# A DeltaNet and max-out kernel on one core: the fourth query tile in a buffer of its own, negations shared by two engines, unread products in the opening, and a last output tile in two halves

## The chip, the cores and the metric

The kernel runs on one core of one Trainium2 chip. The metric is the device time of one execution in microseconds (us), taken as the median of several runs. A profile of one further execution shows what each engine did: PE is TensorE (the matmul engine; PEld is its weight load), DVE is VectorE, ACT is ScalarE, POOL is GpSimd, and SP is the engine that here only starts transfers. A name with a q (SPq, ACTq, POOLq) is the engine's instruction queue at work, mostly starting a transfer (DMA).

## What is computed

```python
# attention block: 4 batches, 8 heads, 768 steps, head size 48
k_n = k / (np.linalg.norm(k, axis=-1, keepdims=True) + 1e-06)
for t in range(S):
    y[:, :, t] = np.einsum('bhd,bhde->bhe', q[:, :, t], state)
    v_old = np.einsum('bhde,bhd->bhe', state, kt)
    state = state + bt[:, :, :, None] * np.einsum('bhd,bhe->bhde', kt, vt - v_old)
# bridge: (B,H,S,D) -> (3072 tokens, 384)
h = np.maximum(np.maximum(x @ w1, x @ w2), x @ w3)     # 384 -> 768
return h @ w_out                                       # 768 -> 384
```

All data is float32. The recurrence over time is strictly sequential; the second block needs the outputs of the first.

## The kernel before

**Tiling.** The 768 steps are cut into 12 chunks of 64 (`NCH`), two chunks make one of six groups (`GROUPS`), and a group gives 512 tokens (`TOK`) for the max-out block. The keys and queries of a chunk come as two tiles n (`load_k(n)`, `load_q(n)`, each two transfers). `turn(n, parts)` transposes a key tile (part 0) or a query tile (part 1) on PE through an identity matrix (L342) and evicts it with one copy (L348, mostly ACT). `gram(n, parts)` multiplies keys with keys or with queries (L419) and evicts with a copy (L430 or L436).

**Recurrence.** Within a chunk the steps are turned into a triangular system. `solve(m)` inverts its diagonal blocks for a whole group on DVE, a long alternation of two small operations (L571, L575). For the first group it ends with a DVE transpose (L583) and copies of the result into the tile `ut` (`placed`, L509), on DVE and ACT. Then PE and the eviction engines alternate for chunk 0: `halves_t` (DVE transposes, L655 and L657), `halves_z` (PE product p_e, copies L698), `halves_u` (PE p_f, negations L710), `turn_t1` (DVE transposes L640, L642), `join_z` (PE p_z, copies L727), `join_u` (PE p_j, negations L738), `new` (PE p_u, copies L786), `to_y` (PE p_y, copies L827), `to_x` (PE p_x, copies L849). For chunk 0 each of these works in two halves of four heads, so that one half is evicted while PE works on the other. `negated_of` names the PSUM tiles and the engine of each negation; for chunk 0 it gives the first half to ACT alone and the second to ACT and DVE, so of the eight negations L710 ACT has six and DVE two, and of the four negations L738 ACT has three and DVE one. `masked` multiplies a `gram` result with the causal mask on DVE (L403). `placed(1, i)` writes the result for chunk 1.

**Max-out block.** `ffn(m)` yields after each small piece; the main loop (L1478, L1531) puts the recurrence of the next group, weight conversion (`weights`: three ACT operations L251 to L253, DVE L263, POOL L267 a piece) and transfers between those pieces. The last groups use fast schemes with fewer products (`crossed_hidden`, `outputs`).

**Order.** All orders are written out by hand (`manual_schedule`), each engine works strictly in the order of the program text, and waits for others by semaphores. The opening is the list of calls from L1314 to L1393. Three query slots exist (`NQ`, the tile `qall`), so `load_q(3)` writes the slot of query tile 0: its transfer stands on POOL's queue behind the first copy of the solve (L546) and waits for `turn(0, (1,))`. `busy(n, of)` (L1306) is already in the kernel: n products of the 128 by 128 identity with itself whose result nobody reads, six before the first transposes, two after `to_y(0)`, one after `to_x(0)`.

**Ending.** `outputs(5, ...)` makes the last four quarter results. The last lines accumulate `p` in eight products and evict it (L1106, stored by SP, L1107), then `q` in two products, evict it (L1110) and store it on both queues (L1111). A store is two transfers of 96 KB.

Of the kernel before, what the change touches and what calls it, by code (L numbers as in the profile page):

```python
# [16 lines left out]
C = 64  # L17
# [6 lines left out]
def kernel(  # L24
# [93 lines left out]
    def rows(bb):  # L118
        return slice(C * bb, C * (bb + 1))
# [18 lines left out]

    def load_k(n, queues=one_queue):
        load(k, kpad[place(n)], n, queues)  # L140

    def load_q(n, queues=one_queue):
        load(q, qpad[n % NQ], n, queues)

    def load_v(c, queue=nc.sync):
        vts[c] = work.tile([128, 2, H, D], FP32, name="v_t", bufs=3)
# [179 lines left out]
    def turn(n, parts=(0, 1), copy=nc.scalar.copy):  # L326

        if n not in kqts:
            if n == 6:
                kqts[n] = work.tile([128, KT, TOK], FP32, name="xt").rearrange(  # L330
                    "p k t -> p (k t)"
                )[:, 0 : NP * 4 * C].rearrange(
                    "p (j b i t) -> p j b i t", b=2, i=2, t=C
                )
            else:
                kqts[n] = work.tile([128, NP, 2, 2, C], FP32, name="kqt", bufs=6)
        kqt = kqts[n]
        p_t = ps_two("p_t")
        for i in parts:
            src = (kpad[place(n)], qpad[n % NQ])[i]  # L340
# [330 lines left out]
    def negated_of(c, name, w):  # L671
        if c:
            p_v = ps_two(name)[:, :, 0 : H * w].rearrange("p g (h x) -> p g h x", x=w)
            yield range(H), (p_v, p_v), (nc.scalar.mul,) * 2
            return
        p = [
            ps_two(name)[:, :, 0 : NP * w].rearrange("p g (h x) -> p g h x", x=w)
            for _ in range(3)
        ]
        yield range(NP), (p[0], p[0]), (nc.scalar.mul,) * 2  # L680
        yield range(NP, H), (p[1], p[2]), (nc.scalar.mul, nc.vector.tensor_scalar_mul)

    def span(hs):
        return slice(hs[0], hs[-1] + 1)
# [294 lines left out]
    def outputs(m, hs):  # L979
# [12 lines left out]
        def times(to, a, b, start=True, stop=True):  # L992
            for g in range(2):
                for j in range(len(a)):
                    nc.tensor.matmul(  # L995
                        to[:, g], a[j][:, 128 * g : 128 * (g + 1)], b[j],
                        start=(start and g == j == 0),
                        stop=(stop and g == 1 and j == len(a) - 1),
                    )

        def x_times(to, lo, right, start=False, stop=True):
            times(
                to,
                [xt[:, KT - 1, lo : lo + 256]],
                [w_sb[0][:, KT - 1, HALF * right : HALF * (right + 1)]],
                start, stop,
            )

        def held(name, dtype_bufs):
# [90 lines left out]
        store(m6, 0, 1)  # L1100
        op(m5, m5, m7, plus)
        yield
        times(p, a22, w["t4"], True, False)
        yield
        x_times(p, 256, 0)
# [2 lines left out]
        yield  # L1108
        x_times(q, 256, 1, True)
        op(m5, m5, q, plus)  # L1110
        store(m5, 1, 1, both_queues)  # L1111
        yield

    thirds, x_sums = {}, {}

    def cross_hidden(i):

# [17 lines left out]
    def crossed_hidden(m, hs):  # L1135

        banks = upper_pool("banks")
        xt, vec = xts[m], nc.vector.tensor_tensor  # L1140
        plus = vec if m == GROUPS - 1 else nc.gpsimd.tensor_tensor
        lo, hi = slice(0, 256), slice(256, 512)
# [153 lines left out]

    conv = weights()
    solving = solve(0)
    zeros(*(t[:, :, :, D:DP] for t in kmore), qall[:, :, :, D:DP])
    for t in (*ut, st):  # L1300
        nc.vector.memset(t, 0.0)
    warm = small("warm", 1)
# [35 lines left out]
    to_blocks(3, (V, A, V, P))  # L1338
    first_blocks()
    load_q(2, (nc.gpsimd, nc.gpsimd))  # L1340
    turn(4, (0,))
    turn(5, (0,))
    some(solving, 1)
    keys(4)
    keys(5)
    turn(6, (0,))
    turn(0, (1,))
    load_q(3, (nc.gpsimd, nc.gpsimd))
    load_beta()
# [228 lines left out]
```

## Time and profile before

| What | Value |
|---|---|
| Median of 3 runs | 502.94 us (501.11 to 507.12) |
| Profiled execution, its own time | 501.88 us |
| Its span, first to last instruction | 500.1 us |
| PE busy | 480.0 us, 96% |
| DVE, ACT, POOL busy | 353.0, 168.3, 189.4 us |
| Mean clock granted to PE | 0.97 |
| Share of PE in the chain that ended last | 85% |

The profile's page gives busy times by engine and the span in 40 slices of 12.5 us. A view by stretches gives the same for stretches of one's own choice with the clock that PE was granted (PEclk, 1.00 is full). A timeline lists instructions in order of time, with the idle time before them in brackets and what ended it. The records of PE count two for each float32 product and one for each transpose.

### The profile page before, as it was taken

Reading aid. Unit: us, or ns where it says so; the run is one execution under the profiler, and the core shown is the slowest. Engines: PE = TensorE matmul, PEld = TensorE weight load, DVE = VectorE, ACT = ScalarE, POOL = GpSimd, SP = SyncE. Lnnn points to the kernel's source line nnn. Section 1 sums busy time; section 2 is a strip of 40 time slices with the busy share of each in tenths; the row PEclk is TensorE's granted clock in tenths of the full one; section 3 lists DMA queues with packets and bytes.
Section 4 is the critical chain, followed back from the end, with each engine's and each line's share of the span. In section 5 each row is a group of like instructions: output and inputs, shape, how many; then the busy total and the mean of one; then the engine's idle time right before and its main releaser. Section 6 shows DMA issues by size and latency. Waiting matters only on the chain.

```text
span 500.1 us, 18762 instructions
## 1 busy us (share of the span) xinstructions
PE 480.0 (96%) x8100; PEld 343.7 (69%) x8100; DVE 353.0 (71%) x829; ACT 168.3 (34%) x323; POOL 189.4 (38%) x313
## 2 busy tenths in 40 slices
PE   7779799999999999999999999999999999999996
PEld 6668678878665555565555565565797457998896
DVE  5888999658697352979552998565998864468753
ACT  5576675985330152200243100252211032213210
POOL 7425596764670394780585870601000020000000
PEclk9657999999999999999999999999999999999999
DMA  8936989873351655544775552833223230330002
GB/s 113 196 64 203 200 171 170 199 208 90 81 144 30 138 122 107 145 130 92 147 138 128 137 135 66 171 54 93 65 68 85 55 72 19 86 91 0 1 16 49
DMA packets 110083, 53.51 MB, mean 107 GB/s; under 512 B 93233, under 2 KB 103889, under 8 KB 110001
## 3 DMA queue, kind: packets, MB, share of 16 engines
q1 hardware_dynamic: 98368, 31.91, 31.7%
q0 software_dynamic: 9088, 19.72, 15.8%
q8 instruction: 64, 1.05, 0.9%
q10 hardware_dynamic: 2544, 0.69, 0.8%
q14 instruction: 19, 0.15, 0.1%
HBM read 39.17 MB, written 13.11 MB: 105 GB/s over the span
## 4 chain that ended last, share of the span: by engine, by line
PE 85%; DMA 6%; ACT 3%; POOL 2%; issue 1%; SPq 1%; DVE 1%; POOLq 0%; ACTq 0%; DVEq 0%
PE p_h L1235 32%; PE p_o L1278 13%; PE p_o L995 13%; PE p_c L1173 5%; PE p_g L419 4%; PE p_u L781 2%; PE p_m L915 2%; PE p_y L823 2%; PE p_k L753 2%; DMA kmore<-in_k_dram 2%; PE p_q L753 2%; PE p_s L804 2%; PE p_j L736 2%; PE p_z L723 1%; DMA qall<-in_q_dram 1%
## 5 line engine op out<-in xcount | busy, mean ns | idle before, releaser
L1235 PE MATMUL p_h<-xt,w_sb 128*128 128x512 f32 (+1 forms) x468 | 176.6, 520 | 1.2 <-POOL w_sb L267 0.8
L1235 PEld LDWEIGHTS p_h<-xt,w_sb 128*128 128x128 f32 x468 | 84.5, 190 | 62.4 <-issue 52.8
L1249 DVE TENSOR_TENSOR h<-h,p_h 128x512 f32<-128x512 f32 (+1 forms) x42 | 23.9, 569 | 54.1 <-PE p_h L1235 51.6
L575 DVE TENSOR_TENSOR y_bl<-y_bl,tmp 128x31 f32<-128x31 f32 (+20 forms) x139 | 50.3, 362 | 4.8
L1278 PE MATMUL p_o<-wo_sb,h 128*128 128x384 f32 x144 | 49.2, 490 | 0.4 <-POOL wo_sb L267 0.4
L571 DVE TENSOR_TENSOR tmp<-x_bl,y_bl 128x31 f32<-128x31 f32 (+20 forms) x139 | 45.9, 331 | 4.1
L377 POOL DMA_DIRECT2D turned<-in_q_dram x72 | 39.1, 551 | 5.5 <-POOL turned L372 2.6
L1245 ACT ACTIVATE h<-p_h 128x512 f32<-128x512 f32 (+1 forms) x30 | 16.6, 552 | 70.6 <-PE p_h L1235 70.5
L1278 PEld LDWEIGHTS p_o<-wo_sb,h 128*128 128x128 f32 x144 | 26.8, 190 | 18.5 <-POOL wo_sb L267 1.0
L267 POOL TENSOR_TENSOR w_sb<-mant,up 128x384 int32<-128x384 int32 x18 | 18.7, 1044 | 34.7 <-DVE mant L263 23.7
L419 PEld LDWEIGHTS p_g<-kqt 48*64 48x64 f32 x1216 | 25.1, 145 | 9.8 <-issue 7.6
L419 PE MATMUL p_g<-kqt 48*64 48x64 f32 (+1 forms) x1216 | 28.5, 245 | 0.9 <-ACT kqt L348 0.8
L1284 ACT COPY o_sb<-p_o 128x384 f32<-128x384 f32 x12 | 5.8, 479 | 61.7 <-PE p_o L1278 54.4
L372 POOL MEMSET turned<- 128x96 f32 x18 | 3.3, 190 | 59.2 <-DVE kqt L393 59.2
L608 POOL DMA_DIRECT2D ut<-y_d x4 | 2.6, 650 | 60.4 <-DMA y_d<-y_bl 60.4
L148 POOL DMA_DIRECT2D v_t<-in_v_dram x14 | 11.6, 830 | 28.7 <-PE p_u L781 28.7
L811 DVE TENSOR_TENSOR st<-st,p_s 48x768 f32<-48x768 f32 (+1 forms) x18 | 17.1, 950 | 7.5 <-PE p_s L804 7.1
L403 DVE TENSOR_TENSOR pt<-p_g,mask 128x512 f32<-128x512 f32 x20 | 13.7, 690 | 10.4 <-PE p_g L419 10.3
L1278 PE MATMUL p_o<-w_sb,xt 128*128 128x384 f32 x60 | 21.0, 486 | 0.0
L765 DVE TENSOR_TENSOR v_t<-v_t,p_k 128x768 f32<-128x768 f32 x11 | 10.5, 950 | 13.8 <-PE p_k L753 13.3
L436 ACT COPY at<-p_g 128x512 f32<-128x512 f32 x22 | 12.8, 585 | 18.5 <-DVE pt L403 16.4
L781 PEld LDWEIGHTS p_u<-v_t,ut 64*64 64x64 f32 x768 | 13.7, 141 | 7.2 <-issue 6.1
(240 smaller groups left out, 916.5 us busy)
## 6 DMA issues: line engine op xcount, KB each, us to landing
w_bits<-in_moe_w_dram SPq DMA_DIRECT2D x9, 384.0 KB, 6.7
w_bits<-in_moe_w_dram POOLq DMA_DIRECT2D x9, 384.0 KB, 4.9
turned<-in_q_dram POOLq DMA_DIRECT2D x72, 48.0 KB, 2.6
out_dram<-o_sb SPq DMA_DIRECT2D x36, 96.0 KB, 2.3
y_x<-y SPq DMA_DIRECT2D x32, 96.0 KB, 2.4
qall<-y_x SPq DMA_DIRECT2D x32, 96.0 KB, 2.8
v_t<-in_v_dram POOLq DMA_DIRECT2D x14, 192.0 KB, 4.4
at_d<-at SPq DMA_DIRECT2D x76, 32.0 KB, 2.5
```

What stands on the lines that cost most here:

```text
L267: nc.gpsimd.tensor_tensor(out=dst.bitcast(I32), in0=mant_v.bitcast(I32), in1=up_v, op=ALU.add)
L377: (queue, nc.gpsimd)[i].dma_start(out=t[p0 : p0 + 32, bb, at : at + NP * 2 * D].rearrange("p (j x) -> p j x", j=NP), in_=(k, q)[i][2 * bb ...
L419: nc.tensor.matmul(p_g[rows(bb ^ (g * i)), par, c0 : c0 + C * (1 + whole)], kq[:, 0], kq if whole else kq[:, i],)
L571: nc.vector.tensor_tensor(out=t_v, in0=row.to_broadcast(t_v.shape), in1=column.to_broadcast(t_v.shape), op=ALU.mult,)
L575: nc.vector.tensor_tensor(out=rest, in0=rest, in1=t_v, op=ALU.subtract)
L753: nc.tensor.matmul(p_b[rows(bb), par, c0 : c0 + D], kqt[g][dims(par), j, bb ^ g, i], st[dims(par), bb ^ g, g, j],)
L781: nc.tensor.matmul(p_v[rows(bb ^ g), g, i], ut[c % NU][rows(bb), g, h], rhs[rows(bb), g, h],)
L995: nc.tensor.matmul(to[:, g], a[j][:, 128 * g : 128 * (g + 1)], b[j], start=(start and g == j == 0), stop=(stop and g == 1 and j == len(a) ...
L1173: nc.tensor.matmul(to, w[stays], moves, start=(n == 0), stop=(n == len(terms) - 1))
L1235: nc.tensor.matmul(p_h, w_sb[i][:, t, f * 128 : (f + 1) * 128], xt[:, t, lo : lo + w], start=(t == 0), stop=(t == KT - 1),)
L1249: nc.vector.tensor_tensor(out=h, in0=h, in1=p_h, op=ALU.max)
L1278: nc.tensor.matmul(p_o, stays, moves, start=(n == 0), stop=(n == len(terms) - 1))
```

## The change

Four edits.

1. Query tile 3 gets a place of its own (`third_q`, 64 columns a head in a buffer of the tile `xt`, cleared at its padding by one more POOL memset), and its two transfers start on POOL's queue right behind those of query tile 2, ahead of the clearing of `y_bl` (L522) and of the copy L546. In the program as built they wait for nothing.
2. For chunk 0 the negations are shared evenly: ACT the first batch pair, DVE the second, in both halves. L710 goes from six on ACT and two on DVE to four and four, L738 from three and one to two and two. `placed(1, 0)`, `masked(pts[0])` and `placed(1, 2)` move: on DVE the order is now the four L710, the transposes of `turn_t1`, `placed(1, 0)`, `masked(pts[0])`, the two L738, `masked(pts[1])`, `placed(1, 2)`.
3. Thirty unread identity products are added in the opening, in ten calls: 4, 1, 1, 1, 8 in the stage of the transposes and Gram products, 3, 3, 4, 3, 2 in the alternation for chunk 0.
4. In the last group the last accumulation is made in two halves `g` of 192 columns, the second in a PSUM bank of its own, with `q` and its store between them; each half is evicted by itself and stored by two transfers of 48 KB, one on SP and one on ACT. The number of products stays.

```diff
+    third_q = work.tile([128, KT, TOK], FP32, name="xt").rearrange(
+        "p k t -> p (k t)"
+    )[:, 0 : H * DP].rearrange("p (h d) -> p h d", d=DP)
+
+    def q_place(n):
+        return third_q if n == 3 else qpad[n % NQ]
...
-        yield range(NP), (p[0], p[0]), (nc.scalar.mul,) * 2
-        yield range(NP, H), (p[1], p[2]), (nc.scalar.mul, nc.vector.tensor_scalar_mul)
+        by_two = nc.scalar.mul, nc.vector.tensor_scalar_mul
+        yield range(NP), (p[0], p[1]), by_two
+        yield range(NP, H), (p[2], p[2]), by_two
...
+        if m == GROUPS - 1:
+            for g in range(2):
+                if g:
+                    p = last_banks[0].tile(
+                        [128, TOK], FP32, name="p_c", tag="one", bufs=6
+                    )[:, 0:DM].rearrange("p (g x) -> p g x", g=2)
+                times(p, a22, w["t4"], True, False, (g,))
+                x_times(p, 256, 0, False, True, (g,))
+                if g == 0:
+                    x_times(q, 256, 1, True)
+                    op(m5, m5, q, plus)
+                    store(m5, 1, 1, both_queues)
+                op(m7[:, g], m7[:, g], p[:, g], plus)
+                for n in range(2):
+                    s0 = (2 * m + 1) * C
+                    both_queues[n].dma_start(
+                        out=out.rearrange("(b s) d -> b s d", s=S)[
+                            2 * n + g, s0 : s0 + C, 0:HALF
+                        ],
+                        in_=m7[rows(n), g],
+                    )
+            return
...
     load_q(2, (nc.gpsimd, nc.gpsimd))
+    load_q(3, (nc.gpsimd, nc.gpsimd))
...
     turn(6, (0,))
+    busy(4, ident)
     turn(0, (1,))
-    load_q(3, (nc.gpsimd, nc.gpsimd))
     load_beta()
     keys(6)
+    busy(1, ident)
     gram(0, (1,), None, later=True)
     turn(7, (0,))
     turn(1, (1,))
+    busy(1, ident)
     keys(7)
     turn(2, (1,))
+    busy(1, ident)
     gram(1, (1,), None, later=True)
...
     gram(3, (1,), None, later=True)
+    busy(8, ident)
     some(solving, HB + 1)
     halves_t(0)
     halves_z(0)
+    busy(3, ident)
     first_norms()
     some(conv, 1)
-    placed(1, 0)
...
     halves_u(0)
+    busy(3, ident)
     turn_t1(0)
+    placed(1, 0)
     join_z(0)
+    busy(4, ident)
     masked(pts[0], by_par(pts[0]))
+    join_u(0)
+    busy(3, ident)
+    masked(pts[1], by_par(pts[1]))
     placed(1, 2)
-    join_u(0)
-    masked(pts[1], by_par(pts[1]))
     old_k(0)
     old_q(0)
     new(0)
+    busy(2, ident)
```

More of the change, by code (lines that the diff above doesn't have):

```diff
@@ L140, in load_k @@
         load(k, kpad[place(n)], n, queues)
+    third_q = work.tile([128, KT, TOK], FP32, name="xt").rearrange(
[3 more added lines that the diff above has]
+        return third_q if n == 3 else qpad[n % NQ]
     def load_q(n, queues=one_queue):
-        load(q, qpad[n % NQ], n, queues)
+        load(q, q_place(n), n, queues)
     def load_v(c, queue=nc.sync):
@@ L339, in turn @@
         for i in parts:
-            src = (kpad[place(n)], qpad[n % NQ])[i]
+            src = (kpad[place(n)], q_place(n))[i]
             for j in range(NP):
@@ L990, in outputs, with times @@
         p, q = (ps_ffn([128, 2, HALF], "p_o") for _ in range(2))
-        def times(to, a, b, start=True, stop=True):
-            for g in range(2):
+        def times(to, a, b, start=True, stop=True, of=(0, 1)):
+            for g in of:
                 for j in range(len(a)):
@@ L996, in times, with x_times @@
                         to[:, g], a[j][:, 128 * g : 128 * (g + 1)], b[j],
-                        start=(start and g == j == 0),
-                        stop=(stop and g == 1 and j == len(a) - 1),
+                        start=(start and g == of[0] and j == 0),
+                        stop=(stop and g == of[-1] and j == len(a) - 1),
                     )
-        def x_times(to, lo, right, start=False, stop=True):
+        def x_times(to, lo, right, start=False, stop=True, of=(0, 1)):
             times(
@@ L1005, in x_times @@
                 [w_sb[0][:, KT - 1, HALF * right : HALF * (right + 1)]],
-                start, stop,
+                start, stop, of,
             )
@@ L1110, in outputs @@
         op(m5, m5, q, plus)
-        store(m5, 1, 1, both_queues)
+        store(m5, 1, 1)
         yield
-    thirds, x_sums = {}, {}
+    thirds, x_sums, last_banks = {}, {}, []
     def cross_hidden(i):
@@ L1139, in crossed_hidden @@
         banks = upper_pool("banks")
+        last_banks.append(banks)
         xt, vec = xts[m], nc.vector.tensor_tensor
@@ L1298 @@
     solving = solve(0)
-    zeros(*(t[:, :, :, D:DP] for t in kmore), qall[:, :, :, D:DP])
+    zeros(*(t[:, :, :, D:DP] for t in kmore), qall[:, :, :, D:DP], third_q[:, :, D:DP])
     for t in (*ut, st):
```

## Prediction

> **What bounds the kernel now.** First the page. PE is busy 96% of the span, and from slice 7 on always; but the first six slices are not full, and the clock row falls there.
>
> ```profile
> span 500.1 us, 18762 instructions
> ...
> PE   7779799999999999999999999999999999999996
> ...
> PEclk9657999999999999999999999999999999999999
> ```
>
> Each digit covers 12.5 us. Past 70 us PE is the bound (30.00 us busy in 70 to 100, 298.65 of 300 in 100 to 400), so a change can gain only in the opening, by bringing the first full stretch forward, or in the ending. Next, the opening by stretches of about 3.41 us, the grid set by the step of the clock at 16.61. Columns: length, busy time and count of PE, PEld, DVE, ACT, POOL, then clock, DMA share, GB/s.
>
> ```profile
> 9.78:13.19 3.41, 2.52 (x92) 2.12 (x88) 3.08 (x6) 2.97 (x7) 3.18 (x7) 1.00 0.42 78
> 13.19:16.61 3.42, 1.84 (x53) 1.40 (x48) 2.71 (x8) 1.82 (x5) 1.12 (x2) 1.00 1.21 184
> 16.61:20.02 3.41, 2.40 (x68) 2.18 (x60) 2.93 (x11) 1.64 (x3) 3.04 (x5) 0.50 1.12 248
> ...
> 37.09:40.50 3.41, 3.09 (x119) 2.82 (x122) 3.30 (x5) 2.39 (x8) 3.30 (x5) 0.50 0.23 70
> 40.50:43.91 3.41, 3.41 (x89) 3.32 (x82) 2.56 (x6) 3.00 (x6) 1.80 (x2) 0.50 0.87 306
> 43.91:47.33 3.42, 3.03 (x18) 2.62 (x17) 3.14 (x10) 2.68 (x6) 1.90 (x3) 1.00 0.74 207
> ```
>
> PE runs at half clock from 16.61 to 43.91, 27.3 us, eight stretches. Busy time doesn't decide it: 3.09 us busy in 37.09 to 40.50 did not raise the clock. What fits all stretches is work counted by the share of the array it fills (my count from the timeline: records times columns, a 64 by 64 tile as a quarter): 0.34 of a full stretch in 13.19 to 16.61, after which the clock falls, 0.34 at most in the seven stretches after it, and 0.37 in 40.50 to 43.91, after which it rises. So small tiles hardly count, full 128 by 128 products do.
>
> Third, DVE's timeline, since in the opening DVE carries the chain and PE waits for it as often as the reverse. Brackets hold idle time and what ended it.
>
> ```profile
> 26.37 2.00 DVE L583 STREAM_TRANSPOSE x_bl<-y_bl 128x1024 f32<-128x1024 f32 x1
> 28.40 1.62 DVE L509 COPY ut<-x_bl 32x512 f32<-32x512 f32 x3
> 30.86 0.71 DVE L655 STREAM_TRANSPOSE t<-ut 128x512 f32<-128x512 f32 x1 [0.84 <-ACT ut L509]
> ...
> 33.48 0.42 DVE L698 COPY z<-p_e 128x256 f32<-128x256 f32 x1 [0.44 <-PE p_e L695]
> ...
> 35.25 0.62 DVE L710 TENSOR_SCALAR ut<-p_f 16x128 f32<-16x128 f32 x2 [0.34 <-PE p_f L706]
> ...
> 37.30 1.54 DVE L403 TENSOR_TENSOR pt<-pt,mask 128x512 f32<-128x512 f32 x1
> ...
> 39.49 0.42 DVE L738 TENSOR_SCALAR ut<-p_j 32x256 f32<-32x256 f32 x1
> 39.94 0.69 DVE L403 TENSOR_TENSOR pt<-pt,mask 128x512 f32<-128x512 f32 x1
> 41.11 0.56 DVE L786 COPY u<-p_u 128x384 f32<-128x384 f32 x1 [0.47 <-PE p_u L781]
> ...
> 42.89 0.56 DVE L827 COPY y<-p_y 128x384 f32<-128x384 f32 x1 [0.32 <-PE p_y L823]
> ```
>
> Up to 28.36 DVE solves without a pause longer than 0.3 us; the clock of PE can't shorten that. After it DVE idles 0.84, 0.44, 0.34, 0.47 and 0.32 us, 2.4 together, and one mask takes 1.54 where the same operation takes 0.69 later. Last, the ending:
>
> ```profile
> 495.46 0.55 DVE L1024 TENSOR_TENSOR up<-up,p_o 128x384 f32<-128x384 f32 x1
> 496.04 0.64 ACTq L1016 DMA_DIRECT2D out_dram<-up  x1
> 496.73 0.59 SPq L1016 DMA_DIRECT2D out_dram<-up  x1
> ```
>
> PE ends at 495.42; SP, which still starts the store before (495.39 to 496.64), starts the last transfer only at 496.73, and it lands at 499.13.
>
> **Part 1, the early query tile.** In before the third query's transfers start at 17.58 and 18.25 and land at 25.54; PE waits 0.86 us for them and turns the tile at 25.68. Now they start at about 13.3, when the second query's issue ends (POOL then clears `y_bl`, 0.98 us, done by 15.8, ahead of the copy L546 at 16.98, so nothing is late; the extra memset, about 0.2 us, stands before POOL's wait of 2.49). With the 7.3 us that the old pair took they land by 21, before PE wants them at about 23.5. The 192 KB then compete with key tile 7 (landed 19.2, PE waits for it 1.01) and query tile 1 (20.5): at 200 GB/s up to 1 us later each. Turn and two Gram products end about 26 instead of 28.68, or 27 with that delay; either is before the solve's end. By itself it frees ACT: its two copies L430 end before 28.36 rather than at 29.76, so its share of L509 runs 28.40 to 30.10 and DVE's wait of 0.84 shrinks to about 0.1: **0.74 us**.
>
> **Part 2, the negations.** DVE gets two more L710 (0.30 each) and one more L738 (0.42): **1.0 to 1.1 us of DVE time added**, on the chain. ACT loses two of 0.27 and one of 0.37, and wins nothing by it that DVE doesn't have to wait for. The moved `placed` and mask cost the same elsewhere. The 1.54 mask ran while POOL copied (L509, 37.26 to 38.29) and ended 0.55 after it; now it comes after four L710, the transposes and one `placed`, by my sum at 36.6, while POOL's copy moves forward with the chain to end near 36.4. If they miss each other, 0.85 is gained; if not, 0. The Trainium skill, Advanced Engine Details and Errata, GPSIMD Details, says that POOL shares SBUF interfaces with DVE operations that have two SBUF inputs; the mask is one, and the row agrees. By that rule either mask may be held again, and the sum would lose this 0.85.
>
> **Part 3, the products.** One is 0.45 us on the slow clock (six from 2.00 to 4.73) and 0.22 on the full one (p_h records of 256 columns follow each other by 0.22). Their places: four where PE waited 1.58 for the query, three in the Gram stage, where PE waited over 2 us for data, eight before the 2.20 us wait for `ut`, fifteen in the alternation, where PE's waits on the full clock are longer than the products before them. At full clock thirty cost 6.6 us of PE time, nearly all in waits. What they buy: with full clock p_e, p_f, p_u and p_y take about half (p_y 1.15 at 68.14 against 2.06 at 40.76), and the four PE waits of DVE (0.44, 0.34, 0.47, 0.32) go: **1.57 us**. About 0.3 returns where PE is late for the last L710.
>
> Opening: 0.74 + 1.57 - 1.05 - 0.3 = 0.96 gained without the mask's 0.85, 1.8 with it. I take 1.5, nearer to the upper, since the second mask, too, finds POOL only starting transfers. After 45 us, weights (w_sb, L267), the second solve and their transfers start from ACT, DVE and POOL instructions of the same chain, so they move along; in 45 to 70 PE idles some 4 us for them, as before.
>
> The Trainium skill, TensorE: Matmul & The Clock Gate, Why this matters for your kernels, warns of PE gaps over about 3 us; by that, rival A below falls away. The trace disagrees: here the clock fell after gaps of 1.58 us at most. The same page, Part 4, says that transposes don't count as PE-busy. Left out of my count, the bound that fits the stretches lies near 0.2 instead of 0.35, the products are ample, and the sum stands; counted, they are scarce, and A's time is as likely.
>
> **Part 4, the ending.** The same number of products ends at the same time. `q` ends five products (0.33 each) earlier, 493.8; its eviction (0.55) and issues (0.64) are done by 495.1, the first half by 495.7. The second half, 192 of 384 columns, is evicted in about 0.35, so its two transfers start near 495.85 on two free queues instead of 496.73, and land in 2.2 to 2.4: 498.1. **1.0 us**, between 0.6 (queues still busy) and 1.1.
>
> **Sum.** 501.88 (the profiled execution, 1.78 around its span) - 1.5 - 1.0 = 499.4. That execution lies 1.06 below the median shown, which itself has 501.11 and 507.12 beside it; the median of the four is 502.4. I add the half microsecond: **499.9**.
>
> **Rivals.**
> A, the clock falls all the same, for one or two stretches. PE is idle between the eight products (25.5 to 27.3) and p_e (30.1); a stretch that lies on this hole holds 0.15 to 0.3 by my count with transposes. Where the grid falls differs from run to run, I suppose. For it: 0.34 was too little at 13.19. Against: the delay of part 1 closes the hole. A stretch on the slow clock costs four products 0.22 more each, 0.9. One or two: 501.2.
> B, slower: the clock falls there and stays down until 44. Then fifteen products take 6.8 us in 30.26 to 43.91, where PE idles 1.6 us on the slow clock. Four stretches cost 3.6 against the opening's 1.5: 499.9 + 3.6 = 503.5. Decides from the third slow stretch on (2.5 gained / 0.9). For it: 3.09 us of small tiles didn't raise the clock. Against: three or four products a stretch add 0.19 to 0.25 to the 0.11 to 0.19 there.
> C, more: both masks run free, no PE wait returns, and weights arrive early: 2.3 in the opening and 1.1: 499.0; where before would lose clock in 45 to 75 too, as the spread of its runs hints, 497.5.
> D, the early query does nothing, since key tile 7 and query tile 1 are late by more than 2 us: 0.74 lost, 500.6.
>
> **How the numbers follow.** Forecast 0.45, A 0.22, B 0.13, C 0.1, D 0.1. The range takes A, B and most of C and the spread of medians: 497.6 to 503.8; the forecast's own is 498.6 to 501. A measurement tells about 1% from no change, 5 us; no case reaches that by itself, only with the runs' spread: faster 0.09, within 0.85, slower 0.06.
>
> **What would show it.** Clock row 1.00 from 16.6 to 44, or short of it by one stretch; query tile 3 turned before 24; DVE's L655 right behind L509, with under 0.2 idle; the first mask under 0.9; the first p_h near 43.8 instead of 45.29; last transfers started before 496 relative to an end of PE at 495.4. A clock of 0.50 across 30 to 44, or p_h at 45.5 or later, proves me wrong in part 3; a mask of 1.5 in part 2.

## The result, and the profile after

The changed kernel is slower: 509.3 us median (507.73 to 511.83) against 503.32 for the kernel before in the same comparison, a ratio of 1.0128 with a 95% interval of 1.009 to 1.0165. A second measurement (a0 below) gave 508.45 against 503.13, 1.0098 (1.0065 to 1.0131). A ratio is not the quotient of the two medians and can differ from it by up to 0.3%. The forecast, 499.9 with a range up to 503.8, is wrong in sign. In the changed kernel line numbers are higher by 7 to 31: L516 is the L509 of before, L718 is L710, L1266 is L1235, and L1340 is the unread product, L1309 before.

The page of the profiled execution after (509.69 us, 1.7 around its span), span, busy time with counts, PE's row and clock row in 40 slices, and two queues:

```profile
span 508.0 us, 18885 instructions
...
PE 490.0 (96%) x8160; PEld 351.8 (69%) x8160; DVE 355.3 (70%) x833; ACT 167.6 (33%) x320; POOL 189.6 (37%) x314
...
PE   7699889999999999999999999999999999999997
...
PEclk9869789998999999999999999999999999999999
...
q1 hardware_dynamic: 98528, 32.01, 31.5%
...
q8 instruction: 64, 1.05, 0.9%
```

The clock row is fuller than before up to 50 us (9869, before 9657), but now dips in slices 5 and 6 (50 to 75 us) and again in slice 10 (112 to 125 us). The last line becomes important below: 64 packets of 16.4 KB are the instructions that one queue brings, one packet for 127.5 of PE's 8160 product records. (Kernels below with 8228 records have 65.)

Where the time went, by when PE starts the first product of each kind in the two profiles (us from the start):

| | before | after | difference |
|---|---|---|---|
| first p_e | 30.88 | 33.89 | +3.01 |
| first p_x | 43.77 | 45.67 | +1.90 |
| first p_h | 45.29 | 47.21 | +1.92 |
| first p_o | 125.98 | 134.91 | +8.93 |
| PE's end | 495.42 | 504.34 | +8.92 |
| the span's end | 500.11 | 507.98 | +7.87 |

So the opening loses 1.9, the loop between 47 and 135 us loses 7.0, the rest nothing, and the ending wins 1.05. The opening first, PE's timeline of the kernel after (start, length, engine and line; in brackets the idle time before and what ended it):

```profile
19.04 0.63 PE L349 MATMUL p_t<-ident,kmore 128*128 128x128 f32 x4 [0.93 <-DMA kmore<-in_k_dram]
22.18 1.08 PE L349 MATMUL p_t<-ident,qall 128*128 128x128 f32 x4 [2.52 <-DMA qall<-in_q_dram]
...
27.22 1.11 PE L349 MATMUL p_t<-ident,xt 128*128 128x128 f32 x4
28.27 1.99 PE L426 MATMUL p_g<-kqt 48*64 48x64 f32 x64
30.18 3.78 PE L1340 MATMUL p_w<-ident 128*128 128x128 f32 x16
33.89 1.33 PE L703 MATMUL p_e<-ut,at 64*64 64x32 f32 x64
35.16 0.94 PE L1340 MATMUL p_w<-ident 128*128 128x128 f32 x6
```

Query tile 1 (`qall`) is late behind the transfers of the early tile (`xt`): PE waits 2.52 us for it and starts at 22.18 instead of 20.56. That the early tile is the cause is likely, not shown: a1 below has the same transfers and turned tile 1 at 20.22. Everything behind moves along; the eight products begin when PE is free, at 30.18, on the half clock, and p_e comes only behind them. DVE after:

```profile
32.45 0.71 DVE L662 STREAM_TRANSPOSE t<-ut 128x512 f32<-128x512 f32 x1 [2.12 <-ACT ut L516]
33.19 1.44 DVE L664 STREAM_TRANSPOSE t<-ut 64x512 f32<-64x512 f32 x2
35.30 0.42 DVE L706 COPY z<-p_e 128x256 f32<-128x256 f32 x1 [0.67 <-PE p_e L703]
...
36.78 0.60 DVE L718 TENSOR_SCALAR ut<-p_f 16x128 f32<-16x128 f32 x2 [0.57 <-PE p_f L714]
37.60 0.29 DVE L718 TENSOR_SCALAR ut<-p_f 16x128 f32<-16x128 f32 x1 [0.22 <-ACT ut L718]
38.23 0.30 DVE L718 TENSOR_SCALAR ut<-p_f 16x128 f32<-16x128 f32 x1 [0.33 <-ACT ut L718]
...
40.49 0.67 DVE L410 TENSOR_TENSOR pt<-pt,mask 128x512 f32<-128x512 f32 x1
```

The wait that was to shrink from 0.84 to 0.1 is 2.12, since ACT turns to L516 only after the late Gram copies. So `ut`, which p_e needs too, is there 1.59 us later than before (32.45 against 30.86), and PE is then still in the eight products: p_e starts another 1.44 later. Together that is the 3.0 us of the table's first row. The mask takes 0.67, as hoped.

Now the loop. By stretches after (length, busy time and count of PE, PEld, DVE, ACT, POOL, clock, DMA share, GB/s), each stretch of full clock with the one behind it:

```profile
51.44:54.85 3.41, 1.60 (x48) 1.38 (x41) 3.31 (x9) 0.99 (x3) 1.98 (x3) 1.00 1.25 201
54.85:58.26 3.41, 3.38 (x91) 2.66 (x93) 2.54 (x9) 2.25 (x6) 3.39 (x4) 0.50 0.70 187
65.10:68.51 3.41, 1.43 (x99) 1.27 (x90) 3.31 (x8) 2.38 (x5) 1.03 (x2) 1.00 0.55 144
68.51:71.92 3.41, 3.41 (x34) 2.31 (x25) 2.61 (x8) 2.26 (x4) 3.41 (x4) 0.50 0.36 113
112.89:116.30 3.41, 2.02 (x70) 1.73 (x70) 1.91 (x4) 1.95 (x5) 2.74 (x4) 1.00 0.39 120
116.30:119.71 3.41, 3.41 (x16) 2.19 (x17) 0.00 (x0) 2.05 (x5) 0.67 (x2) 0.50 0.91 286
```

In the loop before, the clock never left 1.00; here it is halved for 13.65 us (54.85 to 61.68, and the two later stretches), each time behind a stretch in which PE stood still for a part. From the first p_h to the first p_o PE is busy 5.4 us longer than before (half of the 13.65 would be 6.8) and idle 1.6 us longer (5.87 against 4.23); together these are the 7.0. These are the waits of PE in the three stretches of full clock, in its timeline after:

```profile
53.88 2.01 PE L1266 MATMUL p_h<-xt,w_sb 128*128 128x256 f32 x6 [1.81 <-POOL w_sb L274]
...
65.38 0.90 PE L761 MATMUL p_q<-st,kqt 48*64 48x48 f32 x44
68.26 0.70 PE L761 MATMUL p_q<-st,kqt 48*64 48x48 f32 x20 [1.98 <-issue]
...
115.04 0.25 PE L744 MATMUL p_j<-z,t 32*32 32x32 f32 x4 [1.39 <-issue]
```

One wait is for weights; the other two are waits for nothing that the profile names ("issue") in the middle of a group of equal products.

The ending after, in the timeline:

```profile
503.85 0.49 PE L1003 MATMUL p_c<-w_sb,xt 128*128 128x192 f32 x2
504.03 1.22 SPq L1126 DMA_DIRECT2D out_dram<-o_sb  x2
504.04 1.48 ACTq L1126 DMA_DIRECT2D out_dram<-o_sb  x2
504.38 0.35 DVE L1032 TENSOR_TENSOR o_sb<-o_sb,p_c 128x192 f32<-128x192 f32 x1 [0.81 <-PE p_c L1003]
```

Each of the two queues now starts two transfers, the second of them behind the 0.35 us eviction of the last half; from PE's end to the span's end it is 3.64 us instead of 4.69.

### The profile page after: what moved, and what is told of

It is laid out like the page before. It is cut to its first block, busy times and chain, and to the rows that moved or that the text cites. A ratio compares the mean times of both kernels' runs of the same rounds, so it can differ in the third digit from the quotient of the medians.

```text
span 508.0 us, 18885 instructions
## 1 busy us (share of the span) xinstructions
PE 490.0 (96%) x8160; PEld 351.8 (69%) x8160; DVE 355.3 (70%) x833; ACT 167.6 (33%) x320; POOL 189.6 (37%) x314
## 3 DMA queue, kind: packets, MB, share of 16 engines
q8 instruction: 64, 1.05, 0.9%
## 4 chain that ended last, share of the span: by engine, by line
PE 89%; DMA 3%; SPq 2%; issue 2%; POOL 1%; DVE 1%; ACT 1%; POOLq 0%; DVEq 0%
PE p_h L1266 33%; PE p_o L1309 13%; PE p_o L1003 12%; PE p_c L1204 5%; PE p_g L426 4%; PE p_k L761 2%; PE p_m L923 2%; PE p_u L789 2%; PE p_y L831 2%; PE p_q L761 2%; PE p_t L349 2%; PE p_j L744 2%; SPq L129 2%; PE p_z L731 2%; PE p_s L812 1%
## 5 line engine op out<-in xcount | busy, mean ns | idle before, releaser
L1266 PE MATMUL p_h<-xt,w_sb 128*128 128x512 f32 (+1 forms) x468 | 181.0, 532 | 2.5 <-POOL w_sb L274 2.1
L1266 PEld LDWEIGHTS p_h<-xt,w_sb 128*128 128x128 f32 x468 | 87.1, 195 | 64.7 <-issue 53.2
L582 DVE TENSOR_TENSOR y_bl<-y_bl,tmp 128x31 f32<-128x31 f32 (+20 forms) x139 | 52.4, 377 | 4.8
L1309 PE MATMUL p_o<-wo_sb,h 128*128 128x384 f32 x144 | 49.2, 490 | 0.4 <-POOL wo_sb L274 0.4
L1309 PEld LDWEIGHTS p_o<-wo_sb,h 128*128 128x128 f32 x144 | 26.8, 190 | 18.5 <-POOL wo_sb L274 1.0
L1309 PE MATMUL p_o<-w_sb,xt 128*128 128x384 f32 x60 | 21.0, 486 | 0.0
L384 POOL DMA_DIRECT2D turned<-in_k_dram x32 | 17.5, 555 | 1.2 <-POOL turned L379 1.2
```

Source lines behind the costliest of these rows:

```text
L384: (queue, nc.gpsimd)[i].dma_start(out=t[p0 : p0 + 32, bb, at : at + NP * 2 * D].rearrange("p (j x) -> p j x", j=NP), in_=(k, q)[i][2 * bb ...
L582: nc.vector.tensor_tensor(out=rest, in0=rest, in1=t_v, op=ALU.subtract)
L1266: nc.tensor.matmul(p_h, w_sb[i][:, t, f * 128 : (f + 1) * 128], xt[:, t, lo : lo + w], start=(t == 0), stop=(t == KT - 1),)
L1309: nc.tensor.matmul(p_o, stays, moves, start=(n == 0), stop=(n == len(terms) - 1))
```

## The experiments

All medians are in us, all ratios are to the kernel before on the same chip, with 95% intervals; medians of before were 503.0 to 503.5 in every comparison. First the four edits, each alone. Theory P blamed the products, Q the early query tile, G only the place of the grid of 3.41 us in whose steps the clock changes.

**e1_products**, the ten `busy` calls alone:

```diff
+    busy(4, ident)     # ahead of turn(0, (1,)); nine more calls as in the change
```

> The kernel before with the thirty unread products alone (the query of tile 3 still late, negations and ending as before). Theory Q, the early query is the culprit: without it query tile 1 lands at about 20.5 us again, the products keep or restore the full clock, and this kernel is 0 to 2 us faster than before, with p_e starting no later than 31.5. Theory P, the products themselves: the eight run on the slow clock for 3.5 us or more in front of p_e, which starts after 32.5, and the kernel is 3 to 6 us slower. Theory G, only the place of the clock's grid counts: the time scatters by several us from run to run with no clear mean.

506.66, ratio 1.0079 (1.0048 to 1.011): the largest single loss. Its mean granted clock was 0.978 to 0.990 in the six runs, against 0.968 to 0.980 in those of before: the products do raise the clock, and the time rises too. The time lies in P's range (3 to 6 us slower), and p_e started at 34.59, after P's 32.5 (in a profile that starts late, see What stays open).

**e2_query**, query tile 3 in its own place and early:

```diff
+    load_q(3, (nc.gpsimd, nc.gpsimd))     # behind load_q(2, ...), into third_q
```

> The kernel before with the early transfers of query tile 3 alone. Theory Q: query tile 1 lands near 22 instead of 20.5, PE waits 2.5 us for it, the third query is turned no earlier than before, and the kernel is 1.5 to 4 us slower. Theory P: the early tile saves PE its 0.86 us wait and ACT its delay, 0.5 to 1 us faster or the same.

505.02, 1.0036 (1.0014 to 1.0059). In its profile the opening is even (query tile 1 is turned 1.2 us late, at 21.75, but p_x starts at 43.72), and 2.4 us go in the loop, with a pause of 2.54 us in p_k and one stretch of half clock behind it.

**e3_negations**, the shared negations and moved calls:

```diff
+        yield range(NP), (p[0], p[1]), by_two
+        yield range(NP, H), (p[2], p[2]), by_two
```

> The kernel before with the negations shared evenly and the moved copies and masks alone. All theories on the clock: within 1 us of before. If DVE carries the chain, as the prediction had it, 1.05 us of DVE time is added and 0.85 of the held mask may be gained: -0.5 to +1 us. If it is more than 2 us slower, the order on DVE is the culprit.

503.81, 1.0021 (0.999 to 1.0052): not told from zero, and no gain.

**e4_tail** and, on another chip, **e5_tail_again**: the last accumulation in two halves, all else as before.

```diff
+            for g in range(2):
...
+                times(p, a22, w["t4"], True, False, (g,))
```

> The kernel before with the last accumulation in halves alone. The step of the prediction: last transfers start 0.9 us earlier after the same end of PE, 0.6 to 1.1 us faster. Rival: the halves' transfers land as late as the whole ones, 0 to 0.3 us.

> The kernel before with the halved last accumulation alone, once more. Its edit leaves every PE instruction up to the last group in its place, so no limit moves; the two last transfers start some 0.9 us earlier. If that is all: 0.9 to 1.2 us under before, ratio 0.998. If the first result was chance: 1.000.

502.21, 0.9975 (0.9946 to 1.0003), and 503.02, 0.9993 (0.9963 to 1.0023). Both profiles show 3.64 and 3.63 us from PE's end to the span's end, 1.05 less than before; the runs' spread hides it. Since the six times of e1 lie within 506.1 to 508.0, mere scatter by the grid's place (G) is out, and P has the most for it.

Then the products were taken out of the changed kernel, in part or whole.

**a1_no_products**, **a3_no_eight**, **a5_only_eight**: all ten calls out; only the eight ahead of p_e out; all but the eight out.

```diff
-    busy(8, ident)     # a3: this alone; a5: the nine others; a1: all ten
```

> The changed kernel without its thirty products (early query, shared negations and halved ending stay). If the products cost what they cost alone (about 4 us: 506.7 against 503.1), the time is about 505, near the sum of the other three parts alone (503.1 + 1.9 + 0.7 - 0.9 = 504.8). If the early query is the culprit and the products only move the slow stretches, 508 to 509.5. If the parts cost more together than alone, that is if the products' loss needs the other edits, under 503.

> The changed kernel without the eight products ahead of p_e; the other twenty-two stay. If the eight are the cost, because on the slow clock they last 3.78 us and end only at 33.89 where the operand of p_e is there near 33.1, at most some 1 to 1.5 us go in the opening and, if the later lag hangs on that, up to 4: 505 to 508. If the cost lies in the twenty-two (between dependent steps) or in the loop after 47 us by itself, 508.5 to 510. If the clock matters as forecast, it falls for longer in 30 to 44 and the time rises above 510.

> The changed kernel with the eight products alone, the twenty-two others left out. The counterpart of the run without the eight. If the eight carry the cost, 508 to 509.5; if the twenty-two do, about 505, as without any product; if each set costs by its PE time (eight 3.8 us on the slow clock, twenty-two some 7), about 506.5.

a1 505.81, 1.0052 (1.0024 to 1.008); a3 513.01, 1.0189 (1.0139 to 1.0239); a5 507.14, 1.0088 (1.0057 to 1.0118). a1 lies 1.0 us above where the three other edits alone would put it (504.8). The twenty-two cost more without the eight than with them: the eight don't carry the loss, they soften it. a5 fits best the reading that each product costs by its PE time (506.5), but a7 and a8 below speak against it.

**a6_tiny**, the thirty at their places with 16 columns instead of 128:

```diff
-    busy(8, ident)
+    busy(8, ident[:, 0:16])     # and so in the nine other calls
```

> The changed kernel with all thirty products at their places, each 16 columns wide instead of 128, so that PE executes as many instructions in the same order, but they take under half as long and fill an eighth of the array time. If the added instructions themselves cost (the instruction supply of PE, whose unexplained pauses of 1.98 us at 68 us and 1.50 us at 62 us stand in the profiles with products), the time stays at 508 to 510. If the products' duration or what they do to the clock costs, it is that of the kernel without products, about 505, with a slow clock in the opening as long as before the change (over 20 us).

512.52, 1.0186 (1.0144 to 1.0229). A product that does an eighth of the work costs more, not less, which fits neither of the two readings. Part of this lies in the opening, PE's timeline of this kernel:

```profile
29.48 2.56 PE L703 MATMUL p_e<-ut,at 64*64 64x32 f32 x64 [2.15 <-ACT ut L516]
31.96 1.46 PE L1340 MATMUL p_w<-ident 128*128 128x16 f32 x6
33.35 1.93 PE L714 MATMUL p_f<-z,t 64*64 64x32 f32 x64
35.22 1.46 PE L1340 MATMUL p_w<-ident 128*128 128x16 f32 x6
36.61 1.08 PE L731 MATMUL p_z<-ut,at 32*32 32x32 f32 x64
37.61 1.89 PE L1340 MATMUL p_w<-ident 128*128 128x16 f32 x8
```

Without the work the clock stays at half here (27.47 to 47.95), three products of 16 columns still take 1.46, and PE has no pause in which they could sit: from p_e to p_x 18.1 us instead of 12.9. In a3, with full products and the half clock up to 45.19, the same is 16.7. Where the clock is full from p_e on (after: 11.8, e1: 11.5) full products cost nothing there. This is rival B's mechanism, where the clock isn't up.

The other part led to the theory that held. Numbering PE's product records from the start, the pauses without a named cause lie at the same numbers in all profiles: about 977, 1104, 1231, 1358, then 2113, 2240 and 2366; the first four are 127 apart, the share of one instruction packet. Such a number is called a limit below. Theory S: PE's next block of instructions is late there; added instructions shift which group of the loop meets the limit, and a long pause drops the clock. To test it, products were made so small that only their number is left:

```diff
+    def dust(n):
+        p_w = ps_ffn([128, TOK], "p_w")[0:32, 0:16]
+        for _ in range(n):
+            nc.tensor.matmul(p_w, ident[0:32, 0:32], ident[0:32, 0:16])
```

**d1_dust30** (before, `dust` in place of `busy` in the ten calls) and **d2_dust64** (the same with 38 in the first call):

> The kernel before with thirty extra products at the ten places of the change, but each only 32 by 32 by 16, so that PE gets as many instructions and hardly any work. In all profiles so far PE's unexplained pauses lie at the same numbers of its product records (977, 1104, 1231, 1358: one in 127), whatever kernel, only their lengths differ; extra instructions shift which group of the loop meets them. Theory S (the supply of PE's instructions is late at every 127th product, and where such a pause is long the clock falls after it): the loop loses 2 to 4 us as with full products, median 505 to 507, opening unchanged. Theory T (PE time of the products costs): within 0.5 of before, 502.5 to 503.6.

> The same with 34 more of these small products at the first place, 64 in all: 128 records, which puts the limits of 127 on the same groups of the loop as in the kernel before, one limit later. Theory S in its strict form (only the place of the limits counts): as before the change, 503 to 504, and faster than the thirty by 1.5 or more. If the number of instructions costs wherever it stands, it is at least as slow as the thirty; if only PE time costs, both stand near 503, this one up to 1 us later since 64 small products take some 2 us on the slow clock.

d1 509.82, 1.0115 (1.0083 to 1.0147): thirty products without work make the kernel before as slow as the change did. That is more than S had expected (505 to 507), and 3.0 of its profile's loss lie in the opening, for a reason that stays open (see there); 6.0 lie in the loop. In its timeline PE stops at the two places where the changed kernel did, inside p_z and p_q:

```profile
60.35 0.65 PE L723 MATMUL p_z<-ut,at 32*32 32x32 f32 x52 [0.55 <-ACT ut L710]
62.19 0.31 PE L723 MATMUL p_z<-ut,at 32*32 32x32 f32 x12 [1.19 <-issue]
...
64.61 0.90 PE L753 MATMUL p_q<-st,kqt 48*64 48x48 f32 x45
68.03 0.88 PE L753 MATMUL p_q<-st,kqt 48*64 48x48 f32 x19 [2.52 <-issue]
```

d2, with more than twice as many, took 506.87, 1.0072 (1.0038 to 1.0105): faster than the thirty in the median, but intervals overlap and it isn't back at 503 to 504, where S in its strict form had it. In its profile 2.2 of its loss lie in the opening, where small products stand between the steps on the half clock, 1.1 in the loop.

**a7_dust30** (the changed kernel, all thirty as `dust`) and **a8_eight_dust** (the eight full, the rest `dust`):

> The changed kernel with its thirty products cut to 32 by 32 by 16 in place. Without any product it took 505.8, with products of 16 columns on the full array 512.5, as changed 509.3. Theory S: 508 to 510, the excess arising after 47 us at records 1231 and 1358. Theory T (twenty-two products on the slow clock stand 1.5 us each three ahead of the next step, which alone made 5 us of the 512.5): about 506, as without products.

> The changed kernel with the eight full products kept ahead of p_e and the other twenty-two cut to 32 by 32 by 16: the same number of instructions again. Against the eight alone (507.1) it adds instructions without work, against the changed kernel (509.3) it takes away the twenty-two's PE time. Theory S: 508.5 to 510. Theory T: about 507, or 506 if the clock rises early without them.

509.14, 1.0102 (1.007 to 1.0134), and 509.33, 1.0116 (1.0078 to 1.0155). Full or empty, thirty are 509: PE's time for them is not the cost. Both lie in S's range. (a6 lies 3 us above; its profile has 2.0 of that in the opening, where p_h starts at 49.21.)

The last two questions were whether place or number counts, and whether more instructions can repair it. **a9_after_34** is the changed kernel with 34 `dust` in early waits; **d3_dust30_early** and **d4_dust16_early** are the kernel before with 30 and 16 in early waits; **a0_after_again** is the changed kernel itself.

```diff
     turn(6, (0,))
+    dust(8)      # a9, d4; d3: 14
...
     gram(0, (1,), None, later=True)
+    dust(12)     # a9; d3: 8
     turn(7, (0,))
+    dust(14)     # a9 only
...
     gram(3, (1,), None, later=True)
+    dust(8)      # d3, d4
```

> The changed kernel, all of it, and 34 more small products (32 by 32 by 16) in early waits of PE, so that 64 are added in all and the limits of 127 records fall on the groups on which they fell before the change. Theory S: although it executes more, it is faster than the changed kernel by 2 to 4 us, 505 to 507, with the gain after 47 us. If each added instruction costs, or PE time, 509 to 511.

> The kernel before with thirty small products in early waits of PE only (ahead of query tile 0, of key tile 7 and of p_e), none between the dependent steps for chunk 0. Theory S: like the thirty at the places of the change, 507.5 to 510, with pauses in p_z and p_q at records 1231 and 1358. If the place between dependent steps made the 6 us, within 1 of before: 503 to 504.5.

> The same with sixteen small products, 32 records. If every added instruction costs alike, half of the thirty's loss: about 506.5. Theory S in its strict form gives no order by number: the limits then fall 32 records earlier in the loop's groups, and the loss is that of these groups, anything from 503 to 509; a loss far from half of the thirty's speaks for it.

> The changed kernel once more, on the chip of these runs: 508 to 511, with its pauses over 1 us again at records 1358 (in p_q) and 2240 (in p_j) if they belong to the number of the instruction, elsewhere if they belong to the moment.

a9 505.31, 1.0014 (0.998 to 1.0047), where a0 on the same chip has 508.45, 1.0098 (1.0065 to 1.0131): 34 added products make the changed kernel faster, and the intervals don't meet. PE's timeline, first of a0, then of a9:

```profile
60.34 0.32 PE L731 MATMUL p_z<-ut,at 32*32 32x32 f32 x13 [0.93 <-issue]
60.59 1.56 PE L1266 MATMUL p_h<-xt,w_sb 128*128 128x256 f32 x6
62.08 0.75 PE L744 MATMUL p_j<-z,t 32*32 32x32 f32 x64
62.76 0.90 PE L761 MATMUL p_q<-st,kqt 48*64 48x48 f32 x44
66.19 0.88 PE L761 MATMUL p_q<-st,kqt 48*64 48x48 f32 x20 [2.53 <-issue]
67.00 2.93 PE L1266 MATMUL p_h<-xt,w_sb 128*128 128x256 f32 x6
```

```profile
56.16 0.43 PE L761 MATMUL p_k<-st,kqt 48*64 48x48 f32 x10 [0.34 <-issue]
...
61.05 0.62 PE L744 MATMUL p_j<-z,t 32*32 32x32 f32 x38 [0.36 <-ACT z L735]
61.93 0.39 PE L744 MATMUL p_j<-z,t 32*32 32x32 f32 x24 [0.25 <-issue]
62.25 1.15 PE L761 MATMUL p_q<-st,kqt 48*64 48x48 f32 x64
63.33 1.56 PE L1266 MATMUL p_h<-xt,w_sb 128*128 128x256 f32 x6
64.82 0.72 PE L789 MATMUL p_u<-v_t,ut 64*64 64x48 f32 x33
65.82 0.68 PE L789 MATMUL p_u<-v_t,ut 64*64 64x48 f32 x31 [0.28 <-issue]
```

In a0 PE passes a limit at 60.34, has used up the block 3.3 us later and gets the next at 66.19, 5.85 after the limit; the p_h behind it then runs on half clock (2.93 instead of 1.56). In a9 the limits lie elsewhere: the one at 61.93 comes 5.8 us after its forerunner (56.16), since the block between them holds two groups of p_h and PE waited 0.55 us for data in it, and the next costs 0.28.

What PE waits for there can be read from the same traces: they hold the start and the end of every packet of the instruction queue (us from the start).

| pause at record | limit before | packet | PE goes on | behind the packet's end |
|---|---|---|---|---|
| after, 1358 | 62.96 | 65.39 to 66.88 | 68.26 | 1.38 |
| after, 2240 | 109.56 | 112.82 to 113.75 | 115.04 | 1.30 |
| a0, 1358 | 60.34 | 63.34 to 64.83 | 66.19 | 1.36 |
| d1, 1359 | 62.19 | 65.07 to 66.59 | 68.03 | 1.43 |
| e2, 1104 | 50.72 | 55.46 to 57.13 | 58.37 | 1.24 |
| a9, 1485 | 61.93 | 63.01 to 64.39 | 65.82 | 1.42 |

The twenty profiles have 83 pauses of over 0.25 us without a named cause. Of these, 81 end 1.20 to 1.76 us behind the end of an instruction packet, while in the loop the packets come 3.4 to 11 us apart. (The other two, in a7 and a8, stand ahead of query tile 0 and at no limit.) So it is the block of instructions that is late.

d3 took 507.43, 1.0079 (1.0051 to 1.0108), with pauses of 0.96 in p_z and 2.52 in p_q at records 1232 and 1359: place between the steps isn't needed. d4 took 505.93, 1.0065 (1.0032 to 1.0097). Its loss of 2.8 us is about two thirds of that of d3 (4.3), with overlapping intervals, and less than half of that of d1 (6.3), so it decides nothing; its profile loses 1.8 in the opening and 0.8 in the loop.

**b1_late_query_64**, a9 without the early tile, its four products behind `turn(0, (1,))`, to see what remains:

```diff
     turn(0, (1,))
     load_q(3, (nc.gpsimd, nc.gpsimd))
     load_beta()
+    busy(4, ident)
...
+    dust(12)     # behind gram(0, (1,), ...); 22 more behind turn(7, (0,))
```

> The changed kernel without the early query tile, its first four products moved behind the transposes that release the tile's slot, and with 34 small products, so 64 in all as in the run that stood at 505.3. If the early tile costs here what it cost alone: 503 to 504, no better than before. If the rest of the loss was something else, 505 to 506. If the full clock of the opening pays once nothing stands against it, 501 to 502.

502.83, 1.0002 (0.9974 to 1.0031): level with before and in none of the three ranges, with the clock up at 0.992 and 3.4 us of half clock in the opening instead of 27.3. Against a9, on another chip, the median is 2.5 lower, but the ratios differ by 0.0012 alone and both intervals hold 1; so whether the early tile costs anything more once the limits are moved back is not shown. No version beat the kernel before by more than the measurement tells.

The loop, from the first p_h to the first p_o, one profile each:

| products added | kernels | us from p_h to p_o | unexplained pauses at records 1231, 1358, 2240 |
|---|---|---|---|
| none | before, e3, e4, e5 | 80.7, 81.0, 81.0, 81.9 | before and e5: none over 0.25; e3: -, 1.32, -; e4: 0.33, -, - |
| none, query early | a1, e2 | 82.9, 83.1 | a1: -, 1.62, -; e2: -, 0.71, - (and 1.18 and 2.54 at 1104) |
| 30 | e1, d3, a8, d1, a0, a7, a6, after | 83.9, 85.8, 86.0, 86.7, 87.0, 87.2, 87.4, 87.7 | 0.26 to 1.50, 0.58 to 2.80, 1.08 to 1.70 |
| 22, 8, 16 | a3, a5, d4 | 87.8, 84.4, 81.5 | a3: 0.79, 1.03, -; a5: -, 1.43, -; d4: -, 1.12, - |
| 64 | a9, d2, b1 | 81.3, 81.8, 82.6 | a9: 0.34, 0.25, -; d2: 2.00, -, -; b1: 0.33, 1.09, - |

Eight kernels with thirty products of three sizes at two sets of places all lie above every kernel with none or 64. With none, the limit at 1104 falls into p_k, the one at 1358 into p_u; with 64, those at 1232 and 1485 do; with thirty, the limits cut p_z, p_q and p_j. Long pauses occur with none and 64 too, but they add up to less: all pauses over 0.25 us without a named cause in this stretch make 0.9 to 2.0 us in the profiles with none or 64, 3.8 in the two with the query early, 3.6 to 5.7 with thirty and 2.2 to 3.2 in a3, a5 and d4. A pause and a fall of the clock need not cost much, though: d2 has its 2.00 us and 6.8 us of half clock behind it and loses 1.1.

## Why the prediction was wrong, point by point

**The step that failed** is the last sentence on the opening, by which "after 45 us" everything moves along and "in 45 to 70 PE idles some 4 us for them, as before". The forecast for the loop was 0; it lost 7.0 us after and 6.3 in a0. Products had been costed by their PE time and their place ("nearly all in waits"), not as instructions, and the wait for a block of instructions was put at nothing. That the number of products counts, and not their work, is shown: thirty empty ones cost as much (d1, a7), most of it also ahead of the dependent steps (d3, two thirds of d1 with overlapping intervals), and 34 more give most of it back (a9 against a0). That PE waits for a block of instructions is shown too, by the packets that end 1.20 to 1.76 us before 81 of 83 pauses do. That the number works only by the place of the limits is less sure: d2, with 64 as well, came back only in part. The Trainium skill, Runtime: NRT & Kernel Launch, Instruction fetch mechanics, says the same of size: blocks of 16 KiB, 256 instructions, fetched through a queue of the sequencer's own; the trace agrees with 16.4 KB a packet and 127 pairs of weight load and product. The Trainium skill calls the cost of crossing a block mostly hidden there; the trace shows 2.53 us in a0.

**What a pause costs.** In a0 PE is idle 4.0 us longer in the loop than before (8.22 against 4.23), nearly all of it in pauses without a named cause (4.9 against 0.9), and busy 2.3 us longer, with 6.8 us of half clock: together the 6.3. Behind both long pauses of the kernel after (1.98 and 1.39 us) and with the 2.53 of a0 the clock fell, each time for 3.4 or 6.8 us; behind the 1.43 of a0 at record 2240 it didn't. The prediction's count of work by share of the array did carry over: of 2891 stretches of 3.41 us in all twenty profiles 144 were followed by half clock, and a bound of 0.352 puts all but 27 on the right side; if transposes are left out, over 60 stand on the wrong side of the best bound. So of the prediction's two readings the one that counts transposes fits. By PE's busy time nothing separates: the clock fell after a stretch 100% busy with small products (b1 at 18.4, a count of 0.22) and stayed after one 46% busy (a3 at 55.4, 0.38).

**Part 1**, 0.74 gained: wrong. It allowed query tile 1 "up to 1 us" of delay; it was 1.62, tile 3 was turned at 27.22 and not before 24, and the Gram products ended at 30.26, not 26 to 27. This is half of rival D's cause (key tile 7 wasn't late: 19.04, before 19.28), with a larger price: L662's wait grew to 2.12. Alone the edit lost (1.0036), but in the profiles of e2 and a1 the opening gains or stays even and the loop loses, by pauses of 2.54 and 1.62 us at limits. In a1 query tile 1 is turned in time, without a wait:

```profile
20.22 1.09 PE L349 MATMUL p_t<-ident,qall 128*128 128x128 f32 x4
```

**Part 2**, 1.05 cost and 0.85 back: sizes right (two L718 at 0.30 and one L746 at about 0.4 added; the first mask 0.67 after 1.54), alone not told from zero.

**Part 3 in the opening.** From p_e to p_x 1.11 us were gained (12.89 to 11.78); the sum of the terms that belong there, 1.57 and 0.85 less 1.05 and 0.3, is 1.07. That they agree is in part luck: of DVE's four waits that were to go, two went (0.79), but the other two grew from 0.78 to 1.79 (0.67 before L706; 0.57, 0.22 and 0.33 before L718), and the stretch is shorter also because p_e began 1.44 us after its operand. The eight products filled a wait for 2.3 us, up to 32.45, and then held p_e: the Gram products ended late and the clock was still at half, so they took 3.78 us. First p_h 47.21, where the prediction named 45.5 as the mark of being wrong.

**Part 4**, 1.0: right, 1.02 to 1.06 in the profile of every kernel that has it.

**Sum.** Forecast -1.5 in the opening, 0 in the loop, -1.0 in the ending; measured +1.92, +7.0 and -1.05, which is the 7.87 between the spans. The loss of the opening differs between executions: in a0 the first p_h came 0.7 us after that of before. The clock was at half for four stretches of the opening (20.72 to 34.38) as in rival B, but B's cost, the products on the half clock, met only the eight and two in the Gram stage; it shows whole in a3 and a6. B's 503.5 has the sign, not the cause.

**What stays open.** Not shown is what sets the length of a pause at a limit (0.25 to 2.8 us at the same record) and whether the clock falls after it. Packets begin later where other transfers are dense: of 240 packets for records 978 to 2375, those with the DMA engines over 80% busy in the 2 us behind the limit before began 2.2 us after it (median), those under 60% 0.6 us; but they scatter from -1.2 to 5.6, so this is not the whole cause. In six profiles (a3, a7, a8, d1, e1, e5) PE runs up to 3 us late by 13 us. The clock is first full at 14.4 to 16.8 us there, in the others at 5 to 8, and ahead of that products run at half-clock length (in e1, 64 Gram products take 1.99 us at 11.50 and 1.18 at 15.35). e5 changes nothing in the opening, so the edits are not the cause. PE has mostly made this up by 22, but e5's first p_h still comes at 47.14, 1.9 us after that of before, and that of e3, which starts in time, at 47.55, so one profile tells the length of an opening to no better than about 2 us. The first fall of the clock in the loop after, for two of the four half-clock stretches, followed a wait for weights (1.81), which a0 has too (1.80) without the clock falling.

## What to carry to other kernels

An unread product isn't free because PE waits where it stands: it is an instruction, and where many tiny products run through a block of instructions in 3 us, moving the block's limits can cost more than the wait that the product fills. So after an edit that adds or removes PE instructions, look in the trace for pauses without a releaser ("issue") inside groups of equal products, count records between them, and try a few harmless products more before judging the edit. And a fuller clock row is not yet time: with the products alone (e1) the mean clock rose to 0.978 to 0.990 from 0.968 to 0.980, and the kernel fell behind by 3.6 us.

## What the hardware showed that was not expected

PE stopped at fixed product records, 127 apart, for up to 2.8 us, and went on 1.20 to 1.76 us behind the end of a 16.4 KB packet of instructions. In each row of the table of packets the packet began only after PE had passed the limit before it (1.08 to 4.74 us after), so PE had no more than one block in hand; from limit to limit it took 5.30 us after, 5.85 in a0, 6.76 in a7, but also 3.89 in a9. Three products of a 128 by 128 identity took 1.46 us on the half clock with 16 columns and 1.65 with 128 (a6, a3): the columns hardly matter there.
